# The transposed attention output: from PSUM straight into its two parts, a set at a time, and the softmax sums of a set inverted together

## The chip, the cores and the metric

The kernel runs on one core of a Trainium2 chip. The metric is the device time of one execution in microseconds. Six things work side by side on the core: TensorE (PE in the profile, with its weight loads as PEld), VectorE (DVE), ScalarE (ACT), GpSimd (POOL), SyncE (SP, which here only issues transfers) and the DMA engines. Each engine takes its instructions in the order in which they were written for it, and waits on semaphores for the others.

## What is computed

An attention with a local window of 32 keys to each side and 32 global tokens feeds a first mixture layer (the maximum of three products) and then a second one with routed experts. The change lies in the attention of the local queries. Cut to that:

```python
s_ll = scale * np.matmul(q_l, k_l.transpose(0, 1, 3, 2))      # 2 x 8 heads, 512 local queries, 64 wide
s_ll = np.where(np.abs(pos[:, None] - pos[None, :]) <= 32, s_ll, -1000000000.0)
s_lg = scale * np.matmul(q_l, k_g.transpose(0, 1, 3, 2))      # 32 global keys
a_l = sm(np.concatenate([s_lg, s_ll], axis=-1))               # e / (sum(e) + 1e-09)
out_l = np.matmul(a_l, np.concatenate([v_g, v_l], axis=2))
x = attn_out.transpose(0, 2, 1, 3).reshape(B * S, H * D)      # 1088 rows of 512
h = np.maximum(np.maximum(x @ w1, x @ w2), x @ w3)            # 512 x 768 each
x2 = h @ w_out                                                # then routed experts on x2
```

## The kernel before

**Sets and units.** The attention is cut into 16 sets `m` (a batch, a half of the sequence, a pair of heads). A set has two units, `n = 2m` and `n = 2m + 1` (called `u = 0` and `u = 1`), of 128 queries by two heads. A unit runs through: `u_scores` (PE, tile `s`), `u_max` (DVE, L183: mask, row minimum of the negated scores, tile `sm`), `u_exp` (ACT, L188, which also writes the row sums into `ssum`), `u_recip` (DVE, L192 adds 1e-9 to the unit's two sums, L193 inverts them), `u_trans` and `u_thi` (PE transposes into `pt`, ACT copies to `ph`), `u_pv` (PE, tile `pv`, then DVE scales it by the inverted sums into `xq`, L215) and `x_out`.

**What x_out does.** PE transposes the unit's `xq` into the PSUM tile `px` (128 by 128, L221). ACT copies it to `xs` in SBUF (L224). POOL rounds `xs` into `xh`, the high part of x^T (L226), and writes the rest `xs - xh` into `xl` (L227). The later matmuls work on such pairs of parts: of x^T (`xh`, `xl`), of the weights (`wh`, `wl`) and of h.

**The PSUM tile px.** Its pool `ps_x1` holds a single buffer. The transposed output, the scores of the global queries (`sgp`, from set 5 on, L240) and three tiles of a global quad (`gpt2` L266, `gpv` L277, `gpd` L282) take it in turn, each when the one before it has been read out.

**Who sets the order.** The order is written by hand: a loop over steps `s` from -2 to 37 walks through a string of pieces, one string for `s < 14` and one after it:

```python
SEQ = ('m3 scores glob max m2 w0 trans m1 pv out w1 recip quad exp w2 m0 idle',
       'w0 trans scores max pv out idle exp w1 m3 m0 quad recip m1 m2 w2 glob')
```

In step `s` the pieces stand for unit `s + 2` (`scores`, `max`, `exp`), `s + 1` (`recip`), `s` (`trans`), `s - 1` (`pv`) and `s - 2` (`out`). `glob` launches the global scores `sgp` in odd steps. `quad` carries the global quads one stage further; the quads start in steps 17, 21, 28 and 31, and their stages three, four and five later use `px` (`gpt2`, `gpv`, `gpd`). `m3`, `m0`, `m1`, `m2` are 1, 7, 4 and 2 matmuls of the first mixture layer (tile `h`, L428), which run from step 10 on where x^T and weights are there; DVE takes the running maximum of their results (`hA`, L414). `w0`, `w1`, `w2` are pieces of the splitting of the 64-bit weights: ACT `ca` (L309) and `wh` (L321), DVE L311, L314, L317, L324 and L326, and at its end POOL's `ct - wh` (L327) and `wl` (L328). `idle` are matmuls on an empty tile that keep PE busy.

After the loop, from about 116 us, come the rest of the first mixture layer, still with weights to split, its output layer, the routing and the experts.

Of the kernel before, what the change touches and what calls it, by code (L numbers as in the profile page):

```python
# [7 lines left out]
F32 = mybir.dt.float32  # L8
# [6 lines left out]
ALU = mybir.AluOpType  # L15
# [4 lines left out]
P = 128  # L20
# [26 lines left out]
def tile_block(ctx: ExitStack, tc: tile.TileContext, qk, qg, v, vo, vg, w123, w_out, w_gate, w1, w2, consts, out):  # L47
    nc = tc.nc
# [21 lines left out]
    ap = att.enter_context(tc.tile_pool(name="ap", bufs=2))  # L70
# [43 lines left out]
    ident = cst[:, 0:P]  # L114
# [36 lines left out]
    GCOL = [0, 256, 544, 832]  # L151
# [21 lines left out]
    def u_max(n):  # L173
        m, u = divmod(n, 2)
        half = SETS[m][1]
        mk = mask[:, 0 if half == 0 and u == 0 else (2 if half == 1 and u == 1 else 1), :]
        nm = ap.tile([P, 2], F32, tag="nm", bufs=4, name=f"nm{n}")
        ssum = ap.tile([P, 2], F32, tag="ssum", bufs=4, name=f"ss{n}")
        sm = sms[n % NSM]
        SM[n] = (sm, nm, ssum)  # L180
        ps = PS_.pop(n)
        for j in range(2):
            nc.vector.tensor_tensor_reduce(sm[:, j], ps[:, j, 0:P], mk, scale=-0.125, scalar=3.0e38, op0=ALU.add, op1=ALU.min, accum_out=nm[:, j : j + 1])  # L183
# [4 lines left out]
            nc.scalar.activation(sm[:, j], sm[:, j], AF.Exp, bias=nm[:, j : j + 1], scale=-1.0, accum_out=ssum[:, j : j + 1])  # L188

    def u_recip(n):  # L190
        ssum = SM[n][2]
        nc.vector.tensor_scalar_add(ssum, ssum, 1e-9)  # L192
        nc.vector.reciprocal(ssum, ssum)  # L193

    def u_trans(n):
        sm = SM[n][0]
# [371 lines left out]
    for s in range(-2, NU + 6):  # L568
        live, ahead = 0 <= s < NU, 0 <= s + 2 < NU
        if s == 10:  # L570
            mstream = Stream(moe_stream())
        pull = (lambda n: mstream.pull(n, s)) if mstream else (lambda n: None)
        nw = w_steps.get(s, 0)
        for c_ in SEQ[0 if s < 14 else 1].split():
            if c_ == "scores" and ahead:
                u_scores(s + 2)
            elif c_ == "trans" and live:
                u_trans(s)
                u_thi(s)
            elif c_ == "max" and ahead:  # L580
                u_max(s + 2)
            elif c_ == "recip" and 0 <= s + 1 < NU:
                u_recip(s + 1)
            elif c_ == "pv" and 0 <= s - 1 < NU:
                u_pv(s - 1)
            elif c_ == "out" and 0 <= s - 2 < NU:
                x_out(s - 2)
            elif c_ == "exp" and ahead:
                u_exp(s + 2)
            elif c_ == "idle":  # L590
                warm(idles.get(s, 0))
            elif c_ == "quad":
                if s in GQ:
                    globs.append(g_quad(*GQ[s]))
                globs = [g for g in globs if next(g, StopIteration) is not StopIteration]
            elif c_ == "glob" and ahead and s % 2:
                g_scores((s + 2) // 2)
            elif c_[0] == "w":
                take(ws, (nw + int(c_[1])) // 3)
            elif c_[0] == "m" and c_ != "max":  # L600
                pull(MM[int(c_[1])])

        if s % 2 == 0:
            m = (s + 6) // 2
            if 3 <= m < NSET:
                dma_qk(m)
            if 2 <= m - 1 < NSET:
                dma_v(m - 1)
        if s == 11:
            load_qg(1)  # L610
        if s + 1 in GQ:
            dma_vg(*GQ[s + 1])
        if s == 28:
            routing_start()
        if s == 30:
            nc.sync.dma_start(out.rearrange("(p i) (j c) -> p (i j) c", p=64, c=P), zero[0:64].unsqueeze(1).to_broadcast([64, NT * DM // 64 // P, P]))
# [658 lines left out]
```

## Time and profile before

| | |
|---|---|
| median of 3 timed runs | 359.81 us (359.12 to 360.7) |
| profiled execution, its own time | 356.54 us |
| span of that execution, first to last instruction | 354.8 us |
| mean granted TensorE clock | 0.987 |
| busy: PE, DVE, ACT, POOL | 325.0, 251.9, 183.5, 137.0 us |

The times of the timed runs stand some 3 us above the profiled one. Shares of busy time are averages over stages with different limits: the attention loop fills the first 116 us or so, and only that stretch is touched by the change. In the rows below a line of a timeline gives the start, the duration, the engine, the line of code, the operation with what it writes and reads, and in brackets how long the engine stood idle before it and what ended that. Matmuls are pipelined, so the durations of several can overlap.

### The profile page before, as it was taken

What the parts mean: (1) busy time and instruction counts of PE and PEld (TensorE: products, weight loads), DVE (VectorE), ACT (ScalarE), POOL (GpSimd) and SP (SyncE); (2) the same over time, 40 slices, a digit from 0 to 9 for tenths busy, and PEclk for the clock granted to TensorE, in tenths of its full rate; (3) what the DMA queues carried; (4) which work ended last, traced back from release to release, by engine and by line L of the source; (5) the groups of instructions that cost most, each with busy time, mean ns of one, the idle gap of its engine ahead of it and who ended that gap; (6) DMA issues with size and microseconds to landing.
All of it is one profiled execution on the core that took longest, in us unless ns stands there. A gap on an engine that the chain in (4) does not pass through costs nothing. (4 is left out here: it accounts for less than half of the span.)

```text
span 354.8 us, 8524 instructions
## 1 busy us (share of the span) xinstructions
PE 325.0 (92%) x3119; PEld 270.1 (76%) x3119; DVE 251.9 (71%) x665; ACT 183.5 (52%) x458; POOL 137.0 (39%) x162
## 2 busy tenths in 40 slices
PE   7989778999989999998879999999999999997990
PEld 2445546777778999998779999998987788775670
DVE  2679989975888179898973327867896955559580
ACT  3976658676664233424321113354347964768660
POOL 0377586836667156546660000400013550121121
PEclk9999989999999999999999999999999999999996
DMA  7976667752529513323100033742768997378310
GB/s 259 407 247 251 228 222 255 261 215 77 176 69 228 140 61 87 111 103 119 59 2 0 4 116 135 248 172 67 251 231 267 385 339 256 115 255 276 131 32 11
DMA packets 26294, 60.92 MB, mean 172 GB/s; under 512 B 3019, under 2 KB 8139, under 8 KB 26240
## 3 DMA queue, kind: packets, MB, share of 16 engines
q1 hardware_dynamic: 24640, 55.69, 46.3%
q0 software_dynamic: 1600, 4.54, 3.9%
q8 instruction: 30, 0.49, 0.5%
q14 instruction: 24, 0.20, 0.2%
HBM read 58.50 MB, written 7.47 MB: 186 GB/s over the span
## 5 line engine op out<-in xcount | busy, mean ns | idle before, releaser
L428 PE MATMUL h<-xh,wh 128*128 128x256 f32 (+1 forms) x288 | 85.3, 296 | 5.6 <-DVE hA L414 3.4
L428 PE MATMUL h<-xl,wh 128*128 128x256 f32 (+1 forms) x288 | 84.4, 293 | 0.0
L428 PE MATMUL h<-xh,wl 128*128 128x256 f32 (+1 forms) x288 | 84.0, 292 | 0.0
L428 PEld LDWEIGHTS h<-xh,wh 128*128 128x128 f32 x288 | 54.6, 190 | 7.6 <-DVE hA L414 4.6
L428 PEld LDWEIGHTS h<-xl,wh 128*128 128x128 f32 x288 | 54.8, 190 | 0.9 <-issue 0.7
L428 PEld LDWEIGHTS h<-xh,wl 128*128 128x128 f32 x288 | 54.7, 190 | 0.3 <-issue 0.2
L794 POOL DMA_INDIRECT xg<-x2d,idsall x12 | 14.7, 1229 | 58.6 <-DVE ordf L1150 33.3
L418 POOL TENSOR_TENSOR hTl<-hA,hTh 128x288 fp32r<-128x288 f32 (+1 forms) x18 | 15.0, 834 | 55.1 <-ACT hTh L416 55.1
L832 DVE TENSOR_TENSOR w2l<-rawb,w2h 128x1024 fp32r<-128x1024 f32 x20 | 23.9, 1223 | 12.1 <-ACT w2h L831 11.9
L928 PE MATMUL py<-w2h,hhl 128*128 128x512 f32 x112 | 30.9, 400 | 0.0
L832 DVE TENSOR_TENSOR w1l<-rawb,w1h 128x1024 fp32r<-128x1024 f32 x20 | 23.7, 1222 | 8.6 <-ACT w1h L831 8.6
L711 PE MATMUL x<-hTl,wo_h 128*128 128x256 f32 (+1 forms) x96 | 28.2, 294 | 0.0
L711 PE MATMUL x<-hTh,wo_l 128*128 128x256 f32 (+1 forms) x96 | 27.9, 290 | 0.0
L711 PE MATMUL x<-hTh,wo_h 128*128 128x256 f32 (+1 forms) x96 | 27.8, 290 | 0.0
L188 ACT ACTIVATE sm<-sm,nm 128x128 f32<-128x128 f32 x64 | 25.3, 400 | 4.7 <-DVE nm L183 4.6
L327 POOL TENSOR_TENSOR ct<-ct,wh 128x512 f32<-128x512 f32 x18 | 25.0, 1388 | 6.4 <-DVE cap L324 3.8
L226 POOL CAST xh<-xs 128x128 fp32r<-128x128 f32 x32 | 13.5, 420 | 36.0 <-ACT xs L224 36.0
L414 DVE TENSOR_TENSOR hA<-hA,h 128x256 f32<-128x256 f32 (+1 forms) x48 | 20.8, 432 | 9.2 <-PE h L428 7.2
L328 POOL TENSOR_TENSOR wl<-ct,ca 128x512 fp32r<-128x512 f32 x18 | 23.9, 1329 | 3.5 <-DVE ca L326 2.3
L416 ACT CAST hTh<-hA 128x256 fp32r<-128x256 f32 (+1 forms) x24 | 10.1, 420 | 29.3 <-DVE hA L414 29.3
L928 PEld LDWEIGHTS py<-w2h,hhl 128*128 128x128 f32 x112 | 20.9, 188 | 4.9 <-ACT hhl L916 0.4
L894 PE MATMUL acc<-w1h,xT 128*128 128x512 f32 x80 | 21.5, 399 | 1.5 <-PEq L995 0.6
(214 smaller groups left out, 757.8 us busy)
## 6 DMA issues: line engine op xcount, KB each, us to landing
rawb<-in_w_dram SPq DMA_DIRECT2D x45, 512.0 KB
raww<-in_w_dram SPq DMA_DIRECT2D x18, 512.0 KB
rawv<-in_v_dram SPq DMA_DIRECT2D x16, 512.0 KB
qk<-in_qk_dram SPq DMA_DIRECT2D x16, 320.0 KB
rawo<-in_w_out_dram SPq DMA_DIRECT2D x6, 512.0 KB
rw<-in_w_dram SPq DMA_DIRECT2D x5, 512.0 KB
out_dram<-zero SPq DMA_DIRECT2D x1, 2176.0 KB
rawg<-in_vo_dram SPq DMA_DIRECT2D x4, 512.0 KB
```

The source lines that it names most:

```text
L188: nc.scalar.activation(sm[:, j], sm[:, j], AF.Exp, bias=nm[:, j : j + 1], scale=-1.0, accum_out=ssum[:, j : j + 1])
L226: nc.gpsimd.tensor_copy(dst[0], xs)
L327: nc.gpsimd.tensor_tensor(tf, tf, hi.bitcast(F32), op=ALU.subtract)
L328: nc.gpsimd.tensor_tensor(lo, tf, b.bitcast(F32), op=ALU.add)
L414: nc.vector.tensor_tensor(hA[:, :T], hA[:, :T], ph[:, :T], op=ALU.max)
L418: eng.tensor_tensor(hl[:, f_, c0 : c0 + T], hA[:, :T], dst.bitcast(F32), op=ALU.subtract)
L428: nc.tensor.matmul(ph[:, :T], lhsT=w_[:, a], rhs=x_[:, c, c0 : c0 + T], start=n == 0, stop=n == 11)
L711: nc.tensor.matmul(po[:, :T], lhsT=w_[:, f, d * P : (d + 1) * P], rhs=h_[:, f_, c0 : c0 + T], start=k == 0, stop=k == 17)
L794: nc.gpsimd.indirect_dma_start(out=xg[t], out_offset=None, in_=src, in_offset=bass.IndirectOffsetOnAxis(ap=IDS[j][0:n, t, 0:1].bitcast(I32 ...
L832: nc.vector.tensor_tensor(l_, raw_of(j, k), h_.bitcast(F32), op=ALU.subtract)
L894: nc.tensor.matmul(ph[0:nt], lhsT=a[:, c], rhs=w_[:, c, sl], start=i == 0, stop=i == 11)
L928: nc.tensor.matmul(py[0:nt], lhsT=a[:, c, a0 : a0 + nt], rhs=w_[:, c], start=i == 0, stop=i == 23)
```

## The change

Three things change. First, `x_out` works on a set instead of a unit: in even steps it does nothing, and in odd steps it transposes both units of a set into one `px` tile of 128 by 256, and ACT copies that straight into `xh`, rounding as it writes. Second, the low part is no longer POOL's: a new function `x_low` has DVE subtract `xh` from `px` (128 by 256, both units at once). It stands at the pieces `recip`, `quad` and `glob`, and what is outstanding is done at the first of these that comes after `out`: at `recip` in the first string, at `quad` in the second. `xs` and both POOL operations are gone. `px` is now free again when DVE's subtraction has read it, where it was free after ACT's copy. Third, the sums of a set's two units lie in one tile, and both DVE operations on them run once a set, at the step where the second unit's sums are there. `xq` gets a fourth buffer, since a unit's output now waits one step longer.

```diff
     def u_recip(n):
-        ssum = SM[n][2]
-        nc.vector.tensor_scalar_add(ssum, ssum, 1e-9)
-        nc.vector.reciprocal(ssum, ssum)
+        m, u = divmod(n, 2)
+        if u == 1:
+            nc.vector.tensor_scalar_add(SS_[m], SS_[m], 1e-9)
+            nc.vector.reciprocal(SS_[m], SS_[m])
...
+    LOW = []
+
     def x_out(n):
+
         m, u = divmod(n, 2)
-        px = ps_x1.tile([P, P], F32, tag="px", name=f"pxq{n}")
-        nc.tensor.transpose(px, PV_.pop(n).rearrange("p j d -> p (j d)"), ident)
-        c0 = GCOL[m // 4] + u * P
-        xs = ap.tile([P, P], F32, tag="xs", name=f"xs{n}")
-        nc.scalar.copy(xs, px)
-        dst = [t[:, m % 4, c0 : c0 + P] for t in (xh, xl)]
-        nc.gpsimd.tensor_copy(dst[0], xs)
-        nc.gpsimd.tensor_tensor(dst[1], xs, dst[0].bitcast(F32), op=ALU.subtract)
+        if u == 0:
+            return
+        px = ps_x1.tile([P, 2, P], F32, tag="px", name=f"pxq{m}")
+        for i in range(2):
+            nc.tensor.transpose(px[:, i], PV_.pop(n - 1 + i).rearrange("p j d -> p (j d)"), ident)
+        c0 = GCOL[m // 4]
+        h_, l_ = [t[:, m % 4, c0 : c0 + 2 * P] for t in (xh, xl)]
+        px = px.rearrange("p u c -> p (u c)")
+        nc.scalar.copy(h_, px)
+        LOW.append((l_, px, h_))
+
+    def x_low():
+
+        for l_, px, h_ in LOW:
+            nc.vector.tensor_tensor(l_, px, h_.bitcast(F32), op=ALU.subtract)
+        LOW.clear()
...
-            elif c_ == "recip" and 0 <= s + 1 < NU:
-                u_recip(s + 1)
+            elif c_ == "recip":
+                x_low()
+                if 0 <= s + 1 < NU:
+                    u_recip(s + 1)
...
             elif c_ == "quad":
+                x_low()
                 if s in GQ:
...
             elif c_ == "glob" and ahead and s % 2:
+                x_low()
                 g_scores((s + 2) // 2)
```

Two places show what this does to the queues. A row gives the line (those of the changed kernel lie 3 to 25 further down), the operation, what it writes and reads, and in brackets the engine or transfer whose semaphore it waits for. The first is step 17 on DVE, between the scaling of unit 16's output (`xq16`) and the next weight piece; `hA0` is a running maximum of the first mixture layer, `gnm00` the maximum of the first global quad, `ca` the weight being split. Before:

```order
L215 TENSOR_TENSOR xq16_1076<-pv16_1067,ss16_896 128x128 [waits PE_49]
L311 TENSOR_SCALAR ca_1034<-ca_1034 128x512 [waits Activation_49]
L414 TENSOR_TENSOR hA0_0_630<-hA0_0_630,h0_0_2_874 128x256
L252 TENSOR_REDUCE gnm00_1098<-sg00_180 128x1
L253 TENSOR_SCALAR gnm00_1098<-gnm00_1098 128x1 [waits DVE_49]
L192 TENSOR_SCALAR ss18_1005<-ss18_1005 128x2
L193 RECIPROCAL ss18_1005<-ss18_1005 128x2 [waits DVE_49]
L314 TENSOR_SCALAR ca_1034<-ca_1034 128x512
```

And now:

```order
L219 TENSOR_TENSOR xq16_993<-pv16_984,ss8_830 128x128 [waits PE_49]
L326 TENSOR_SCALAR ca_952<-ca_952 128x512 [waits Activation_49]
L429 TENSOR_TENSOR hA0_0_584<-hA0_0_584,h0_0_2_808 128x256
L241 TENSOR_TENSOR xl_138<-pxq7_995,xh_137 128x256 [waits Activation_49]
L267 TENSOR_REDUCE gnm00_1014<-sg00_180 128x1
L268 TENSOR_SCALAR gnm00_1014<-gnm00_1014 128x1 [waits DVE_49]
L329 TENSOR_SCALAR ca_952<-ca_952 128x512
```

The two operations on the sums of unit 18 are gone here, and the subtraction that empties `px` (`pxq7`, set 7) stands behind the weight piece and the maximum. On PE in the same step the launch of the global scores of set 9 (`sgp9`) stands behind matmuls of `h`, before:

```order
L428 MATMUL h1_0_0_927<-xh_137,wl1_798 128x256
L428 MATMUL h1_0_1_1107<-xh_137,wh1_797 128x256
L428 MATMUL h1_0_1_1107<-xl_138,wh1_797 128x256
L428 MATMUL h1_0_1_1107<-xh_137,wl1_798 128x256 [waits Pool_49]
L240 MATMUL sgp9_1112<-qk9_809,qg1_745 64x2x160 [waits Activation_49]
L199 MATMUL pt18_1115<-cst_116,sm0_124 128x128 [waits PE_49]
```

And now:

```order
L443 MATMUL h1_0_0_855<-xh_137,wl1_736 128x256
L443 MATMUL h1_0_1_1021<-xh_137,wh1_735 128x256
L443 MATMUL h1_0_1_1021<-xl_138,wh1_735 128x256
L443 MATMUL h1_0_1_1021<-xh_137,wl1_736 128x256 [waits Pool_49]
L255 MATMUL sgp9_1026<-qk9_747,qg1_689 64x2x160 [waits DVE_49]
L203 MATMUL pt18_1029<-cst_116,sm0_124 128x128 [waits Activation_49]
```

The instructions stand alike; `sgp9` waited for ACT (the copy of `px`) and now waits for DVE (the subtraction).

The second place is step 31 on DVE, from the last sums to the weight pieces behind; `ca_` and `ct_` are two weights in the splitting, `xq30` the scaled output of unit 30. Before:

```order
L192 TENSOR_SCALAR ss31_1955<-ss31_1955 128x2
L193 RECIPROCAL ss31_1955<-ss31_1955 128x2 [waits DVE_49]
L326 SCALAR_TENSOR_TENSOR ca_1798<-raww31_1376,ca_1798 128x512
L311 TENSOR_SCALAR ca_2027<-ca_2027 128x512 [waits Activation_49,Pool_49]
L314 TENSOR_SCALAR ca_2027<-ca_2027 128x512 [waits DVE_49]
L215 TENSOR_TENSOR xq30_2079<-pv30_2070,ss30_1887 128x128 [waits PE_49]
L317 SCALAR_TENSOR_TENSOR ct_2087<-raww32_1725,ca_2027 128x512 [waits DMAHW2_49,DVE_49]
L252 TENSOR_REDUCE gnm11_2109<-sg11_1251 128x1
L253 TENSOR_SCALAR gnm11_2109<-gnm11_2109 128x1 [waits DVE_49]
L414 TENSOR_TENSOR hA2_0_1992<-hA2_0_1992,h2_0_1_2046 128x256 [waits PE_49,Activation_49,Pool_49]
```

And now:

```order
L196 TENSOR_SCALAR ss15_1751<-ss15_1751 128x4
L197 RECIPROCAL ss15_1751<-ss15_1751 128x4 [waits DVE_49]
L341 SCALAR_TENSOR_TENSOR ca_1666<-raww31_1271,ca_1666 128x512
L326 TENSOR_SCALAR ca_1875<-ca_1875 128x512 [waits Activation_49]
L329 TENSOR_SCALAR ca_1875<-ca_1875 128x512 [waits DVE_49]
L219 TENSOR_TENSOR xq30_1927<-pv30_1918,ss15_1751 128x128 [waits PE_49]
L332 SCALAR_TENSOR_TENSOR ct_1933<-raww32_1599,ca_1875 128x512 [waits DMAHW2_49,DVE_49]
L241 TENSOR_TENSOR xl_138<-pxq14_1929,xh_137 128x256 [waits Activation_49]
L267 TENSOR_REDUCE gnm11_1956<-sg11_1155 128x1
L268 TENSOR_SCALAR gnm11_1956<-gnm11_1956 128x1 [waits DVE_49]
L429 TENSOR_TENSOR hA2_0_1846<-hA2_0_1846,h2_0_1_1894 128x256 [waits PE_49,Pool_49]
```

The subtraction for set 14 (`pxq14`) stands behind four weight pieces and `xq30`. On PE in that step the fifth transpose of the third global quad (`gpt210`) takes `px`. Before:

```order
L428 MATMUL h2_0_1_2046<-xh_137,wh2_1178 128x256
L428 MATMUL h2_0_1_2046<-xl_138,wh2_1178 128x256
L428 MATMUL h2_0_1_2046<-xh_137,wl2_1179 128x256
L428 MATMUL h2_0_2_2096<-xh_137,wh2_1178 128x256 [waits DVE_49]
L265 MATMUL gpt10_2098<-cst_116,sg10_980 128x128 [waits Activation_49]
L265 MATMUL gpt10_2098<-cst_116,sg10_980 128x128 x3
L266 MATMUL gpt210_2099<-cst_116,sg10_980 32x128 [waits Activation_49]
L428 MATMUL h2_0_2_2096<-xl_138,wh2_1178 128x256
```

And now:

```order
L443 MATMUL h2_0_1_1894<-xl_138,wh2_1086 128x256
L443 MATMUL h2_0_1_1894<-xh_137,wl2_1087 128x256
L443 MATMUL h2_0_2_1942<-xh_137,wh2_1086 128x256 [waits DVE_49]
L280 MATMUL gpt10_1945<-cst_116,sg10_904 128x128 [waits Activation_49]
L280 MATMUL gpt10_1945<-cst_116,sg10_904 128x128 x3
L281 MATMUL gpt210_1946<-cst_116,sg10_904 32x128 [waits DVE_49]
L443 MATMUL h2_0_2_1942<-xl_138,wh2_1086 128x256
L443 MATMUL h2_0_2_1942<-xh_137,wl2_1087 128x256
```

`gpt210` waited for ACT and now waits for DVE, with everything behind it on PE.

## Rows read from the trace of the kernel before

**Rows 1.** Windows: busy us of each engine with instructions, granted clock, DMA share, GB/s.
```profile
40.00:50.00 10.00, 7.05 (x122) 4.53 (x122) 8.44 (x31) 7.21 (x27) 6.56 (x9) 0.92 0.64 228
50.00:60.00 10.00, 8.95 (x149) 6.30 (x141) 9.59 (x33) 6.87 (x24) 8.51 (x11) 0.91 0.94 321
60.00:70.00 10.00, 10.00 (x160) 8.00 (x160) 9.40 (x33) 7.70 (x27) 7.33 (x10) 1.00 0.61 201
```

**Rows 2.** Groups by line, 8 to 125 us: shapes, count | busy, mean ns | idle before.
```profile
L227 POOL TENSOR_TENSOR xl<-xs,xh 128x128 fp32r<-128x128 f32 x32 | 17.2, 537 | 2.6
L226 POOL CAST xh<-xs 128x128 fp32r<-128x128 f32 x32 | 13.5, 420 | 36.0 <-ACT xs L224 36.0
L192 DVE TENSOR_SCALAR ss<-ss 128x2 f32<-128x2 f32 x31 | 9.4, 303 | 0.3 <-ACT sm L188 0.2
L193 DVE RECIPROCAL ss<-ss 128x2 f32<-128x2 f32 x31 | 5.1, 166 | 1.1
L204 ACT COPY ph<-pt 128x256 f32<-128x256 f32 x32 | 11.8, 369 | 1.2 <-PE pt L199 0.7
L414 DVE TENSOR_TENSOR hA<-hA,h 128x256 f32<-128x256 f32 x12 | 5.0, 413 | 0.9 <-PE h L428 0.7 <-ACT hA L412 0.2
```

**Rows 3.** Timeline, steps 7 to 9: a weight piece on POOL, DVE behind it, PE.
```profile
22.88 1.27 POOL L328 TENSOR_TENSOR wl<-ct,ca 128x512 fp32r<-128x512 f32 x1
22.94 1.49 DVE L311 TENSOR_SCALAR ca<-ca 128x512 f32<-128x512 f32 x1
25.00 0.45 PE L171 MATMUL s<-qk 64*32 64x128 f32 x16 [1.34 <-DVE nm L183]
27.14 0.16 DVE L192 TENSOR_SCALAR ss<-ss 128x2 f32<-128x2 f32 x1
27.22 0.27 ACT L224 COPY xs<-pxq 128x128 f32<-128x128 f32 x1 [0.19 <-PE pxq L221]
```

**Rows 4.** Timeline, steps 14 and 15: the sums on DVE, the global scores on PE.
```profile
44.56 1.23 DVE L192 TENSOR_SCALAR ss<-ss 128x2 f32<-128x2 f32 x1
47.73 0.75 PE L240 MATMUL sgp<-qk,qg 128*64 128x320 f32 x2 [2.01 <-ACT xs L224]
```

**Rows 5.** Timeline, steps 17 and 18: global scores on PE, DVE, the next px.
```profile
54.39 0.75 PE L240 MATMUL sgp<-qk,qg 128*64 128x320 f32 x2 [0.29 <-ACT xs L224]
54.71 0.29 DVE L215 TENSOR_TENSOR xq<-pv,ss 128x128 f32<-128x128 f32 x1
55.71 0.41 DVE L414 TENSOR_TENSOR hA<-hA,h 128x256 f32<-128x256 f32 x1
57.01 0.33 PE L221 MATMUL pxq<-cst,xq 128*128 128x128 f32 x1 [0.76 <-ACT sg L243]
```

**Rows 6.** Timeline, step 21 (first quad's gpv) and step 27 (global scores).
```profile
68.27 0.65 PE L277 MATMUL gpv<-rawg,gph 128*32 128x64 f32 x32
68.39 0.42 DVE L414 TENSOR_TENSOR hA<-hA,h 128x256 f32<-128x256 f32 x1
91.45 0.41 DVE L414 TENSOR_TENSOR hA<-hA,h 128x256 f32<-128x256 f32 x1
91.76 0.75 PE L240 MATMUL sgp<-qk,qg 128*64 128x320 f32 x2
```

**Rows 7.** Timeline, step 31: DVE's weight pieces, gpt2 and the next pv on PE.
```profile
103.39 1.50 DVE L311 TENSOR_SCALAR ca<-ca 128x512 f32<-128x512 f32 x1
104.16 0.27 PE L266 MATMUL gpt<-cst,sg 128*32 128x128 f32 x1
106.23 0.28 DVE L215 TENSOR_TENSOR xq<-pv,ss 128x128 f32<-128x128 f32 x1
106.43 0.68 DVE L317 SCALAR_TENSOR_TENSOR ct<-raww,ca 128x512 int32<-128x512 int32 x1
106.56 0.43 PE L213 MATMUL pv<-rawv,ph 128*32 128x64 f32 x16 [1.42 <-DVE xq L215]
```

**Rows 8.** Waits after the loop, 116 to 190 us: who for whom, total us, times, longest.
```profile
DVE hA L414 <- PE h L428: 6.0, 5, 2.8
```

More of the change, by code (lines that the diff above doesn't have):

```diff
@@ L88, in tile_block @@
     SETS = [(b, half, hp) for b in range(B) for half in range(2) for hp in range(4)]
-    raws, K, V, VG, W, SG_, PV_, PS_, PT_, SM, hT = {}, {}, {}, {}, {}, {}, {}, {}, {}, {}, {}
+    raws, K, V, VG, W, SG_, PV_, PS_, PT_, SM, hT, SS_ = {}, {}, {}, {}, {}, {}, {}, {}, {}, {}, {}, {}
     def dma_qk(m):
@@ L177, in u_max @@
         nm = ap.tile([P, 2], F32, tag="nm", bufs=4, name=f"nm{n}")
-        ssum = ap.tile([P, 2], F32, tag="ssum", bufs=4, name=f"ss{n}")
+        if u == 0:
+            SS_[m] = ap.tile([P, 2, 2], F32, tag="ssum", bufs=4, name=f"ss{m}")
+        ssum = SS_[m][:, u]
         sm = sms[n % NSM]
@@ L213, in u_pv @@
                 nc.tensor.matmul(po[32 * g : 32 * g + 32, j], lhsT=ph[:, j, 32 * g : 32 * g + 32], rhs=V[m][:, 4 * u + g, 64 * j : 64 * j + 64], start=True, stop=True)
-        xq = ap.tile([P, 2, 64], F32, tag="xq", bufs=3, name=f"xq{n}")
+        xq = ap.tile([P, 2, 64], F32, tag="xq", bufs=4, name=f"xq{n}")
         nc.vector.tensor_tensor(xq, po, SM.pop(n)[2].unsqueeze(2).to_broadcast([P, 2, 64]), op=ALU.mult)
         PV_[n] = xq
+    LOW = []
     def x_out(n):
         m, u = divmod(n, 2)
-        px = ps_x1.tile([P, P], F32, tag="px", name=f"pxq{n}")
-        nc.tensor.transpose(px, PV_.pop(n).rearrange("p j d -> p (j d)"), ident)
-        c0 = GCOL[m // 4] + u * P
-        xs = ap.tile([P, P], F32, tag="xs", name=f"xs{n}")
-        nc.scalar.copy(xs, px)
-        dst = [t[:, m % 4, c0 : c0 + P] for t in (xh, xl)]
-        nc.gpsimd.tensor_copy(dst[0], xs)
-        nc.gpsimd.tensor_tensor(dst[1], xs, dst[0].bitcast(F32), op=ALU.subtract)
+        if u == 0:
+            return
[11 more added lines that the diff above has]
+        LOW.clear()
     def g_scores(m):
```

## The prediction

> **What bounds the kernel now.** I read the windows over the attention loop first [rows 1]. From 40 to 60 us DVE is busy 8.44 and then 9.59 of every 10 us and PE only 7.05 and 8.95: DVE sets the pace, and PE stands and waits. PE's granted clock is 0.92 and 0.91 there. From 60 us on PE is busy 10.00 of 10: now PE sets the pace, and any new stop of PE is paid in full. Then the groups by line [rows 2]: POOL's two operations per unit are 32 times 0.420 and 0.537 us, but POOL stood idle 36.0 us waiting for ACT before them. They are on nobody's path by themselves. What they can cost is indirect. Adding 1e-9 to two numbers on DVE (L192) takes 0.303 us in the mean and inverting the same two (L193) 0.166; one of the former took 1.23 us [rows 4]. Some DVE operations stand still while POOL works. So I looked for places where such a stop reached PE [rows 3, 4], and then for the places where PE will have to wait for DVE's new operation [rows 5 to 7].
>
> **What the change adds and removes, engine by engine.** POOL loses 13.5 + 17.2 = 30.7 us. DVE loses 16 pairs on the sums, 16 x (0.303 + 0.166) = 7.5 us, and gains 16 subtractions of 128 by 256 with one operand in PSUM. The nearest row is the running maximum of the same shape and sources, 0.413 us [rows 2], so 16 x 0.41 = 6.6 us: nearly even. ACT exchanges two copies of 0.27 us [rows 3] for one of 128 by 256, 0.369 us by L204 [rows 2], and gains 16 x 0.17 = 2.7 us that nobody waits for. PE makes the same transposes, two in a row. No transfer is issued, moved or removed. So the change is not about amounts of work but about who waits for whom.
>
> The subtraction could itself stand behind POOL. I take 0.41 for it, since L414's mean of 0.413 was taken with POOL busy beside it [rows 2]; as a bound, L192's excess over L193, 0.14 us, would come on top at each of the two places that count below, 0.3 us together. The Trainium skill (SBUF — State Buffer, Who interferes with whom) says that a VectorE instruction with at most one input in SBUF and outside the two-port modes does not contend with GpSimd, while a `tensor_scalar` can. The trace agrees (0.413 for L414, 1.23 for one L192); by the rule the sum stays as it is, without it 0.3 us are added.
>
> **The terms.** I go through the loop in time.
>
> *Step 8, a gain.* A weight piece on DVE started at 22.94, just after POOL's last weight operation (22.88, 1.27 us), took 1.49 us, and PE's next scores waited 1.34 us for DVE's maximum behind it [rows 3]. On POOL this weight stood behind `xh` and `xl` of unit 4; without their 0.42 + 0.54 us it ends before DVE comes. I take -1.2 us; the bounds are -1.34 and 0.
>
> *Steps 5 to 9, a loss.* At s = 9 DVE reaches the place where the subtraction now stands at 27.14, but ACT's copy starts at 27.22 [rows 3]. A copy of 0.37 us ends at 27.6 or later, so DVE waits some 0.45 us that it did not wait before, with the maximum of unit 11 queued behind it. DVE enters its busy stretch that much later: +0.5 us, between 0 (PE and ACT have other waits to hide it) and 1.5 (three such steps).
>
> *Steps 10 to 16, even.* At s = 15 no matmul of h stands between the transposes and `sgp`, and PE already waits 2.01 us for ACT [rows 4]. Now DVE's 0.41 us come behind ACT's copy: +0.5. Against it stands the L192 of 44.56 us, 0.9 us above its mean [rows 4], which held the chain that ACT waited for; with POOL's weight operations earlier I count half of that, -0.5. Together 0; bounds -2.0 (the whole wait goes) and +1.0.
>
> *Step 17, the first new stop.* `sgp` started at 54.39. DVE scaled `xq` only at 54.71 and took its maximum from 55.71 to 56.12 [rows 5]; the subtraction stands behind both, so it ends at 56.5 and `sgp` starts 2.1 us later. Of that comes back the 0.76 us which PE waited at 57.01 for `px` [rows 5], since even steps have no transposes now, and some 0.6 us because POOL's pieces leave DVE earlier. +0.8; bounds 0 and 2.1.
>
> *Steps 21 and 27.* `gpv` started at 68.27; the maximum that now stands ahead of the subtraction ran from 68.39 to 68.81, so `px` is free at 69.2, 0.95 us late. At s = 27 it is 91.86 + 0.41 = 92.3 against 91.76, 0.5 us [rows 6]. PE arrives later by the term above, and DVE follows PE only in part, so I take +0.5 for both; bounds 0 and 1.45. The other odd steps have DVE there in time.
>
> *Step 31, the largest.* `gpt2` ran at 104.16. The subtraction of that step stands behind three weight pieces (the second one, at 103.39, lasted 1.50 us beside POOL), `xq` at 106.23 and a fourth piece that ended at 107.11 [rows 7]. It ends at 107.5, and PE, in order, stands from 104.2 to 107.5. Part of this PE lost anyway, 1.42 us before the `pv` at 106.56 [rows 7]; but the matmuls between `gpt2` and that `pv`, which filled 104.16 to 105.14, now come after the stop: `pv` starts at 107.5 + 1.0 = 108.5 instead of 106.56, +1.9 us, less 0.2 for the transpose that step 32 no longer has. +1.7; lower bound 0.4, if DVE's pieces slip past POOL's without being held.
>
> Nothing gives this back later: after the loop DVE waits 6.0 us for PE's products [rows 8], so both engines carry a delay of PE on together.
>
> **Sum.** -1.2 + 0.5 + 0 + 0.8 + 0.5 + 1.7 = +2.3 us on the profiled execution's 356.54 us. That execution lies 3.3 us below the median of the timed runs; on their scale 359.81 + 2.3 = 362.1 us.
>
> **The rivals.** *First, the relief wins (faster).* If POOL's weight operations come so early that DVE runs ahead of PE through 40 to 60 us, the waits of 1.34, 2.01 and 0.76 us go [rows 3 to 5], 4.1 together, while the new stops shrink to 0.4 at step 31 and some 0.5 elsewhere: -3.2 us, 356.6. It decides at step 17: DVE must have done its subtraction by 54.4, over 2 us earlier than its queue allows now. For it speaks that DVE's long pieces all lie beside POOL's; against it that these are POOL's weight operations, which stay, and that small ones were only a part.
>
> *Second, no difference.* POOL's operations were hidden, DVE's amount is even, and PE's stops at 17 to 27 are filled by DVE's being earlier; then -1.2 and +1.7 remain with small change, about 360.3 us. This is also what happens if the relief does not come and the stops are shorter than I read them.
>
> *Third, the clock.* The granted clock was 0.92 and 0.91 in the windows around the 2.01 us wait of step 15 [rows 1, 4], that is, PE spent some of it at the lower of its two levels, 0.8 + 0.9 = 1.7 us lost. The new stops of 2.1 us at step 17 and 3.3 us at step 31 are as long or longer; one more such loss each gives 363.8 to 365.5 us, say 365. Against it: that the wait made the clock fall is read only from the two standing side by side, and PE had little else to do around that step, which is not so at 17 and 31. The Trainium skill (TensorE: Matmul & The Clock Gate, HAM oscillation) describes kernels in which each pause of PE throws its clock back to 1.2 GHz; by it this rival's 365 would hold, while the windows here show one such stretch in the loop.
>
> **How the numbers follow.** Forecast 0.50, with its own range of 360 to 364; relief 0.17; no difference 0.20; clock 0.13. Predicted is the forecast, 362.1 us. The range has to reach into the second and third rival: 357.8 to 366.0 leaves out most of the first, about 0.13, and a little above. A run of this kernel tells changes of about 0.5% (1.8 us) from none. Faster by more than that: the first rival, 0.17. Within it: the second mostly and the forecast's low end, 0.26. Slower: the rest, 0.57.
>
> **What would show it.** The profile after should have PE waiting for `xl` (the subtraction) at `sgp` of step 17 and, above all, some 3 us at `gpt2` near 104 us; no wait of the scores near 25 us; DVE's sums at half their count. If `gpt2` does not wait, the largest term falls and with it the sign; if PE's granted clock falls again behind step 17 or 31, the third rival holds; if DVE's subtractions start as soon as ACT's copies end from step 11 on, the first.

## The result, and the profile after

The changed kernel takes 364.44 us (median of 15 runs, 361.49 to 368.67); the kernel before, run in turn with it, 359.36 us (355.29 to 363.79). The ratio is 1.0137, 95% interval 1.0105 to 1.017: some 4.9 us slower. Single executions of one kernel differ by over 2%, so below all verdicts come from ratios of timed runs, and of a profiled execution only the order, the waits and the durations of single instructions are read. The ratios take only the executions within 1.5% of the quickest of their kernel, which leaves three of twelve for the run in which POOL subtracts from a second copy of ACT's.

First the windows over the attention loop of the kernel after (busy us of each engine with instructions, granted clock, DMA share, GB/s), to be laid beside [rows 1]:

```profile
30.00:40.00 10.00, 8.25 (x95) 5.43 (x94) 9.90 (x23) 5.03 (x20) 5.22 (x4) 0.83 0.65 226
40.00:50.00 10.00, 7.69 (x145) 5.09 (x143) 9.50 (x32) 7.68 (x26) 4.30 (x4) 1.00 0.65 228
50.00:60.00 10.00, 7.92 (x139) 5.83 (x136) 8.80 (x34) 6.79 (x23) 4.58 (x4) 1.00 0.92 324
60.00:70.00 10.00, 8.53 (x118) 6.81 (x117) 9.74 (x31) 7.50 (x26) 5.98 (x5) 1.00 0.53 197
```

PE (the first number after the window's length) was busy 10.00 of 10 us from 60 to 70 us; now it is busy 8.53 there, at the full clock of 1.00. DVE (the third) is no less busy there than before, 9.74 against 9.40. Who stops PE is told by its waits, 8 to 125 us (who for whom, total us, times, longest), of after:

```profile
PE sgp L255 <- DVE xl L241: 5.0, 3, 2.0
PE s L171 <- DVE nm L186: 2.8, 4, 1.5
PE gpt L281 <- DVE xl L241: 2.6, 1, 2.6
PE gpv L292 <- issue: 1.5, 1, 1.5
```

and the two largest of before:

```profile
PE s L171 <- DVE nm L183: 3.2, 3, 1.3
PE sgp L240 <- ACT xs L224: 2.3, 2, 2.0
```

PE waited nowhere for the low part of x^T before; now it waits 7.6 us for `xl`, in four places, and the 1.5 us at `gpv` will turn out to be a fifth. The groups by line of after, 8 to 125 us (shapes, count | busy, mean ns | idle before), answer to [rows 2]:

```profile
L241 DVE TENSOR_TENSOR xl<-pxq,xh 128x256 fp32r<-128x256 f32 x16 | 6.7, 420 | 2.2 <-ACT xh L235 1.9
L341 DVE SCALAR_TENSOR_TENSOR ca<-raww,ca 128x512 f32<-128x512 uint32 x12 | 12.2, 1017 | 0.0
L342 POOL TENSOR_TENSOR ct<-ct,wh 128x512 f32<-128x512 f32 x12 | 16.7, 1390 | 39.5 <-DVE ca L339 32.9 <-ACT wh L336 6.6
```

The subtraction takes 0.42 us. The new number is the second line: a weight piece on DVE takes 1017 ns, where before it took 817:

```profile
L326 DVE SCALAR_TENSOR_TENSOR ca<-raww,ca 128x512 f32<-128x512 uint32 x12 | 9.8, 817 | 0.0
```

And POOL now stands idle ahead of its weight operation (third line of after) until DVE has done its part, 32.9 us in all; before, it came there from its small operations, and the idle time was 0.4 us.

Where the time goes is best read from the starts of `pv`, the product that PE does once per unit (unit n is scaled in step n + 1). Each column is a kernel's start minus that of before, in us, from the timelines:

| unit | 0 | 7 | 8 | 11 | 16 | 17 | 18 | 20 | 21 | 26 | 27 | 30 | 31 | span |
|---|---|---|---|---|---|---|---|---|---|---|---|---|---|---|
| after | +0.58 | +0.98 | -0.01 | +2.30 | -0.85 | +0.94 | +0.05 | +0.08 | +1.73 | +1.75 | +3.05 | +3.02 | +4.43 | +5.0 |

The losses that stay come at three places: between units 20 and 21 (step 21), 26 and 27 (step 27), 30 and 31 (step 31). The timeline of after (start us, duration us, engine, line, instruction, in brackets the idle time before it) at step 21:

```profile
67.38 1.30 POOL L342 TENSOR_TENSOR ct<-ct,wh 128x512 f32<-128x512 f32 x1 [0.70 <-DVE ca L339]
67.58 0.28 DVE L219 TENSOR_TENSOR xq<-pv,ss 128x128 f32<-128x128 f32 x1
67.73 0.36 ACT L235 CAST xh<-pxq 128x256 fp32r<-128x256 f32 x1
67.78 1.45 DVE L341 SCALAR_TENSOR_TENSOR ca<-raww,ca 128x512 f32<-128x512 uint32 x1
69.15 0.41 DVE L429 TENSOR_TENSOR hA<-hA,h 128x256 f32<-128x256 f32 x1
69.48 0.41 DVE L241 TENSOR_TENSOR xl<-pxq,xh 128x256 fp32r<-128x256 f32 x1
70.00 0.65 PE L292 MATMUL gpv<-rawg,gph 128*32 128x64 f32 x32 [1.47 <-issue]
```

and the same place before:

```profile
67.79 0.68 DVE L326 SCALAR_TENSOR_TENSOR ca<-raww,ca 128x512 f32<-128x512 uint32 x1
67.97 0.66 POOL L226 CAST xh<-xs 128x128 fp32r<-128x128 f32 x1 [0.39 <-ACT xs L224]
68.70 0.46 POOL L227 TENSOR_TENSOR xl<-xs,xh 128x128 fp32r<-128x128 f32 x1
69.11 1.29 POOL L327 TENSOR_TENSOR ct<-ct,wh 128x512 f32<-128x512 f32 x1
```

ACT has read `px` by 68.09, but the buffer is still owed a reading by DVE. On DVE that reading stands behind a weight piece, which lasts 1.45 us instead of 0.68 because POOL's long operation started 0.40 us ahead of it; before, POOL still had its two small ones to do, and the long one came at 69.11, when DVE's piece was over. So `gpv` starts at 70.00, right after the subtraction, and not at 68.27 [rows 6]: +1.73 us. Step 27 repeats it:

```profile
92.19 1.29 POOL L342 TENSOR_TENSOR ct<-ct,wh 128x512 f32<-128x512 f32 x1 [3.88 <-DVE ca L339]
92.58 1.45 DVE L341 SCALAR_TENSOR_TENSOR ca<-raww,ca 128x512 f32<-128x512 uint32 x1
93.95 0.41 DVE L429 TENSOR_TENSOR hA<-hA,h 128x256 f32<-128x256 f32 x1
94.29 0.41 DVE L241 TENSOR_TENSOR xl<-pxq,xh 128x256 fp32r<-128x256 f32 x1
94.84 0.72 PE L255 MATMUL sgp<-qk,qg 128*64 128x320 f32 x2 [1.15 <-DVE xl L241]
```

And step 31, with the largest single stop, which answers to [rows 7]:

```profile
106.11 0.37 ACT L235 CAST xh<-pxq 128x256 fp32r<-128x256 f32 x1 [0.30 <-PE pxq L231]
108.13 1.54 DVE L332 SCALAR_TENSOR_TENSOR ct<-raww,ca 128x512 int32<-128x512 int32 x1
109.60 0.41 DVE L241 TENSOR_TENSOR xl<-pxq,xh 128x256 fp32r<-128x256 f32 x1
110.07 0.29 PE L281 MATMUL gpt<-cst,sg 128*32 128x128 f32 x1 [2.61 <-DVE xl L241]
```

ACT is done with `px` at 106.48; DVE comes to it 3.12 us later.

### The profile page after: what moved, and what is told of

It is laid out like the page before. It is cut to its first block, busy times and chain, and to the rows that moved or that the text cites. A ratio compares the mean times of both kernels' runs of the same rounds, so it can differ in the third digit from the quotient of the medians.

```text
span 359.8 us, 8419 instructions
## 1 busy us (share of the span) xinstructions
PE 327.7 (91%) x3119; PEld 272.4 (76%) x3119; DVE 249.9 (69%) x649; ACT 182.7 (51%) x442; POOL 108.7 (30%) x98
## 5 line engine op out<-in xcount | busy, mean ns | idle before, releaser
L443 PE MATMUL h<-xh,wh 128*128 128x256 f32 (+1 forms) x288 | 86.4, 300 | 4.4 <-ACT hA L427 2.2
L443 PE MATMUL h<-xl,wh 128*128 128x256 f32 (+1 forms) x288 | 85.6, 297 | 0.0
L443 PE MATMUL h<-xh,wl 128*128 128x256 f32 (+1 forms) x288 | 85.3, 296 | 0.0
L443 PEld LDWEIGHTS h<-xh,wh 128*128 128x128 f32 x288 | 55.4, 192 | 6.4 <-DVE hA L429 3.1
L433 POOL TENSOR_TENSOR hTl<-hA,hTh 128x288 fp32r<-128x288 f32 (+1 forms) x18 | 15.8, 878 | 85.7 <-ACT hTh L431 85.7
L429 DVE TENSOR_TENSOR hA<-hA,h 128x256 f32<-128x256 f32 (+1 forms) x48 | 20.8, 432 | 11.2 <-PE h L443 9.3
L186 DVE CUSTOM_DVE_ANT_0 sm<-s,mask 128x128 f32<-128x128 f32 x64 | 15.9, 286 | 12.3 <-PE s L171 12.0
```

The costliest lines, as they stand in the source:

```text
L429: nc.vector.tensor_tensor(hA[:, :T], hA[:, :T], ph[:, :T], op=ALU.max)
L433: eng.tensor_tensor(hl[:, f_, c0 : c0 + T], hA[:, :T], dst.bitcast(F32), op=ALU.subtract)
L443: nc.tensor.matmul(ph[:, :T], lhsT=w_[:, a], rhs=x_[:, c, c0 : c0 + T], start=n == 0, stop=n == 11)
```

## The experiments

The theory after this reading ("release"): `px` has one buffer, and it comes free when its last reader is done. The change makes DVE the last reader, and DVE comes late, since the subtraction stands behind weight pieces in its queue. One rival ("realignment"): the relocated work only shifts which operations meet, and any stop taken away comes back elsewhere. A second one: POOL's freedom is the cause, since its long operations now start beside DVE's weight work. A third: the sums that are inverted together cost time.

**The two parts apart.** The paired sums alone, with x^T as before:

```diff
-        ssum = ap.tile([P, 2], F32, tag="ssum", bufs=4, name=f"ss{n}")
+        if u == 0:
+            SS_[m] = ap.tile([P, 2, 2], F32, tag="ssum", bufs=4, name=f"ss{m}")
+        ssum = SS_[m][:, u]
...
-        ssum = SM[n][2]
-        nc.vector.tensor_scalar_add(ssum, ssum, 1e-9)
-        nc.vector.reciprocal(ssum, ssum)
+        m, u = divmod(n, 2)
+        if u == 1:
+            nc.vector.tensor_scalar_add(SS_[m], SS_[m], 1e-9)
+            nc.vector.reciprocal(SS_[m], SS_[m])
```

> The kernel before with the paired softmax sums alone; the x^T of a unit goes as before through ScalarE and GpSimd. Both theories (the px buffer held by VectorE's subtraction; GpSimd's products running beside VectorE's weight work) put the loss into the other part of the change, so this alone should be 0.994 to 1.004 of the kernel before, with no wait of TensorE for VectorE on px. If the pairing itself (a sum that has to wait for the second unit's exponentials) carries the loss, 1.008 or more, with xq or nm late on VectorE.

Measured: 0.992 (0.9881 to 0.9959), 356.3 us where before had 359.22. It is faster than both kernels. The third rival falls. In its waits of PE, the wait for DVE's maxima is down from 3.2 us to 0.6:

```profile
PE s L171 <- DVE nm L185: 0.6, 1, 0.6
```

Its timeline shows the wait of step 8 [rows 3] go although POOL has all its work:

```profile
22.69 0.78 DVE L314 TENSOR_SCALAR ca<-ca 128x512 f32<-128x512 f32 x1
23.26 1.34 POOL L331 TENSOR_TENSOR wl<-ct,ca 128x512 fp32r<-128x512 f32 x1
```

DVE's piece starts 0.57 us ahead of POOL's operation and lasts 0.78 us; in [rows 3] it started 0.06 us behind it and lasted 1.49.

The other part alone, x^T through ACT and DVE with the sums unit by unit:

```diff
-        if u == 0:
-            SS_[m] = ap.tile([P, 2, 2], F32, tag="ssum", bufs=4, name=f"ss{m}")
-        ssum = SS_[m][:, u]
+        ssum = ap.tile([P, 2], F32, tag="ssum", bufs=4, name=f"ss{n}")
...
-        m, u = divmod(n, 2)
-        if u == 1:
-            nc.vector.tensor_scalar_add(SS_[m], SS_[m], 1e-9)
-            nc.vector.reciprocal(SS_[m], SS_[m])
+        ssum = SM[n][2]
+        nc.vector.tensor_scalar_add(ssum, ssum, 1e-9)
+        nc.vector.reciprocal(ssum, ssum)
```

> The other half of the change alone: x^T of a set through ScalarE and VectorE as in the changed kernel, the softmax sums unit by unit as before. If the two parts simply add (sums alone 0.992, both 1.014): 1.018 to 1.026. If the sums' gain was already lost in the changed kernel, because the px waits sit where it had been, 1.010 to 1.016, as the changed kernel itself.

Measured: 1.0248 (1.0199 to 1.0296). As far as the intervals tell, the parts simply add: 0.992 x 1.0248 = 1.0166, within the interval of the whole change. So one half of the change gains some 0.8% and the other loses some 2.5%.

**Other buffers for the tiles that waited.** In the changed kernel, three tiles of the quads (the two `gpv` of the first batch element, and the `gpt2` of step 31) move from `px` to the buffer of `pt`:

```diff
-        pt2 = ps_x1.tile([P, P], F32, tag="px", name=f"gpt2{b}{quad}")
+        pt2 = (ps_t.tile([P, P], F32, tag="pt", name=f"gpt2{b}{quad}") if (b, quad) == (1, 0) else ps_x1.tile([P, P], F32, tag="px", name=f"gpt2{b}{quad}"))
...
-        pv = ps_x1.tile([P, 64], F32, tag="px", name=f"gpv{b}{quad}")
+        pv = (ps_t.tile([P, 64], F32, tag="pt", name=f"gpv{b}{quad}") if b == 0 else ps_x1.tile([P, 64], F32, tag="px", name=f"gpv{b}{quad}"))
```

> The changed kernel with three tiles of the global quads (gpt2 of the third, gpv of the first two) in the PSUM buffer of pt instead of px. Theory 'release': the waits of gpv at step 21 (1.47 us) and of gpt2 at step 31 (2.61 us, of which 1.4 cost something) go, 2.5 to 3.1 us less than the changed kernel, ratio 1.004 to 1.008. Theory 'realignment': no difference from the changed kernel, ratio 1.011 to 1.016.

Measured: 1.0031 (0.9983 to 1.0078) against 1.0137 for the changed kernel: no room for realignment's 1.011, and by its middle a little more gained than release expected. At step 21 of its timeline everything on DVE is as it was in the changed kernel, the piece of 1.45 us and the late subtraction, but `gpv` doesn't wait for it:

```profile
68.71 1.45 DVE L341 SCALAR_TENSOR_TENSOR ca<-raww,ca 128x512 f32<-128x512 uint32 x1
69.38 0.65 PE L292 MATMUL gpv<-rawg,gph 128*32 128x64 f32 x32
70.41 0.41 DVE L241 TENSOR_TENSOR xl<-pxq,xh 128x256 fp32r<-128x256 f32 x1
```

This also shows that the 1.5 us which the profile put down to "issue" at `gpv` were a wait for `px`. The control is the same move in the kernel before:

> Control: the kernel before with the same three quad tiles moved from px into the pt buffers. If the move gained in the changed kernel because VectorE no longer stops it there, it has nothing to gain here: 0.997 to 1.004. If the move is a gain of its own (px was short of buffers in both kernels), 0.986 to 0.993, as much as it gained there.

Measured: 1.0031 (0.9986 to 1.0076): nothing to gain there. The move gains only where DVE holds `px`.

Moving the global scores `sgp` instead, into the buffers of `h`, for all sets where before only the first five used them:

```diff
-        pool, tag = (ps_mm, "mm") if m < 5 else (ps_x1, "px")
+        pool, tag = (ps_mm, "mm")
```

> The changed kernel with all global scores sgp in the buffers of the h products instead of px. Theory 'release': the waits of sgp at steps 15, 17 and 27 (1.78, 2.04, 1.15 us) go; the first two stand in a stretch that DVE paces, so only step 27 and a little of 17 comes back, 1.2 to 2 us, ratio 1.008 to 1.011. Theory 'realignment': ratio 1.011 to 1.016.

Measured: 1.0158 (1.0088 to 1.0229), a miss for release and within realignment's range. Its waits of PE say where the time went:

```profile
PE sgp L255 <- DVE hA L429: 3.2, 2, 1.9
PE gpt L281 <- DVE xl L241: 2.6, 1, 2.6
```

`sgp` doesn't wait for `xl` any more; it waits for DVE all the same, since the buffers of `h` are let go by DVE's running maxima (L429). At step 17 one queue's lateness was exchanged for the same queue's lateness: 1.85 us of stop where there were 2.04. At step 27 the stop did go, but a new one of 1.31 us came at step 29, and that one goes back to a transfer: the DVE work ahead of the maximum stood behind a wait for a table of constants, 2.63 us where the changed kernel waited 0.99 for it.

```profile
101.43 0.23 DVE L145 CAST iota_b<-iota 128x128 bf16<-128x128 f32 x1 [2.63 <-DMA iota<-in_consts_dram]
```

So this run doesn't tell what the move of `sgp` is worth without that wait. Both moves together:

> Both moves together: px is used by x^T and gpd alone. Theory 'release': 4 to 5 us less than the changed kernel, ratio 0.998 to 1.003. Theory 'realignment': ratio 1.011 to 1.016.

Measured: 1.007 (1.0029 to 1.0112), between the two expectations and not better than the quads alone; the wait of 2.63 us for the constants and the stop of 1.31 us at step 29 are there as well.

**Who lets px go.** ACT makes a second copy of `px` into SBUF, and POOL subtracts from that; DVE has no part in x^T:

```diff
+        xs = ap.tile([P, 2 * P], F32, tag="xs", name=f"xs{m}")
         nc.scalar.copy(h_, px)
-        LOW.append((l_, px, h_))
+        nc.scalar.copy(xs, px)
+        nc.gpsimd.tensor_tensor(l_, xs, h_.bitcast(F32), op=ALU.subtract)
```

> The changed kernel, but ACT makes a second copy of px into SBUF and POOL subtracts from that, so px is free after ACT and DVE has no subtraction. Theory 'release' (px held by DVE's subtraction stops PE at steps 17, 21, 27 and 31): the stops of 2.04, 1.47, 1.15 and 2.61 us go, the kernel comes back to within 1.5 us of the kernel before (ratio 0.997 to 1.004). Theory 'realignment' (with POOL's small operations gone the rest of POOL's work falls on DVE's pieces at worse moments): POOL's work is back only in half, the loss of 5 us shrinks by half at most (ratio 1.006 to 1.013).

Measured: 0.9911 (0.9834 to 0.9987). The loss of the x^T part is gone, and realignment's 1.006 to 1.013 lie outside the interval. That interval is wide and reaches into release's range, so how much of the gain of the sums is left this run doesn't tell. Its longest wait of PE is for ACT again, as before:

```profile
PE sgp L257 <- ACT xs L237: 2.7, 1, 2.7
```

With the quads' move on top of it:

> The kernel with the low part by GpSimd from a second copy of ScalarE's (0.991), with the three quad tiles moved into the pt buffers as well. As px is no longer held there, the move has nothing left to gain: 0.986 to 0.996. If the quad tiles want buffers of their own whoever reads px, 0.980 to 0.986.

Measured: 0.9947 (0.9908 to 0.9986): nothing more to gain from other buffers once DVE doesn't hold `px`. And with POOL making both parts from one copy, the division of work of before but 128x256 at a time:

```diff
-        nc.scalar.copy(h_, px)
-        LOW.append((l_, px, h_))
+        xs = ap.tile([P, 2 * P], F32, tag="xs", name=f"xs{m}")
+        nc.scalar.copy(xs, px)
+        nc.gpsimd.tensor_copy(h_, xs)
+        nc.gpsimd.tensor_tensor(l_, xs, h_.bitcast(F32), op=ALU.subtract)
```

> x^T of a set in one tile, as in the changed kernel, but by the engines of before: ScalarE copies px once into SBUF, GpSimd makes the high part and the low part from the copy, 128x256 each; the sums paired. px is let go by one copy of ScalarE's. If only the reader that lets px go counts: 0.986 to 0.996, near the kernel with the paired sums alone (0.992). If working by the set is a cost of its own (the transposes of two units wait for the later one): 1.000 or more.

Measured: 0.9974 (0.9934 to 1.0013). It falls between the two expectations. Against the paired sums alone (0.992) working by the set may cost half a per cent, but the two intervals overlap, and more this run doesn't say.

The run made to part the buffer from DVE's work leaves DVE its subtraction and takes only `px` from it:

```diff
+        xs = ap.tile([P, 2 * P], F32, tag="xs", name=f"xs{m}")
         nc.scalar.copy(h_, px)
-        LOW.append((l_, px, h_))
+        nc.scalar.copy(xs, px)
+        LOW.append((l_, xs, h_))
```

> The changed kernel with one edit: ScalarE makes a second copy of px, into SBUF, and VectorE subtracts from that copy. VectorE keeps its 16 subtractions at the same places in its queue and GpSimd stays free of them; only px is now let go by ScalarE. If the px buffer held by the queued subtraction is the cause: no wait of TensorE for xl is left, and the ratio is 0.988 to 0.999. If VectorE's added work, or GpSimd's products beside its weight work, is the cause by itself: 1.008 or more.

Measured: 1.0061 (1.002 to 1.0102), between the two. No wait of PE for `xl` is left, as release wants. But the test was not clean. From SBUF eight of the 16 subtractions are lengthened, all beside an operation of POOL's (the other eight take 0.42 or 0.43 us): 802 ns in the mean where the changed kernel has 420, 16 x 0.38 = 6.1 us more on DVE. Three groups of weight pieces give some of it back (their means fall from 772 to 648, from 563 to 485 and from 1017 to 943 ns, 3.5 us together), so DVE's work grew by less; PE's waits for DVE's maxima grew from 2.8 to 4.4 us. The group of the subtraction, and one of the long ones in the timeline:

```profile
L243 DVE TENSOR_TENSOR xl<-xs,xh 128x256 fp32r<-128x256 f32 x16 | 12.8, 802 | 5.3 <-ACT xs L237 5.2
...
44.25 1.27 POOL L345 TENSOR_TENSOR wl<-ct,ca 128x512 fp32r<-128x512 f32 x1 [0.69 <-DVE ca L343]
44.48 1.33 DVE L243 TENSOR_TENSOR xl<-xs,xh 128x256 fp32r<-128x256 f32 x1 [0.37 <-ACT xs L237]
```

**The place in the queue, and POOL.** The subtraction issued directly after ACT's copy, ahead of the weight piece:

```diff
         LOW.append((l_, px, h_))
+        x_low()
```

> The changed kernel with the subtraction issued directly after ScalarE's copy, ahead of the weight piece that stood before it in VectorE's queue at steps 9, 17, 21 and others. If the place in the queue is what made px late: the waits of TensorE for xl at steps 21 and 27 (1.47 and 1.15 us) fall under 0.5, the ratio is 1.002 to 1.009. If VectorE now stands idle at the head of its queue until ScalarE's copy comes (some 0.5 to 0.6 us a set from the end of xq to the end of the copy, on 16 sets): 1.012 to 1.020, with the idle time before xl put to ACT xh.

Measured: 1.0047 (0.9999 to 1.0095): two thirds of the loss are gone. At step 21 the order is turned round:

```profile
68.30 0.42 DVE L242 TENSOR_TENSOR xl<-pxq,xh 128x256 fp32r<-128x256 f32 x1
68.64 0.90 DVE L342 SCALAR_TENSOR_TENSOR ca<-raww,ca 128x512 f32<-128x512 uint32 x1
68.78 0.65 PE L293 MATMUL gpv<-rawg,gph 128*32 128x64 f32 x32 [0.26 <-DVE xl L242]
```

From unit 20 to 21 it loses 0.44 us and from 26 to 27 0.11, where the changed kernel lost 1.65 and 1.30. The weight piece itself gains too, as it comes later against POOL's operation: 0.90 us, and over all twelve 735 ns in the mean where it was 1017. So this run moves two things at once, the release of `px` and the meeting with POOL. Of what it still loses, 1.07 us is a stop at step 29, where the subtraction stands behind the wait for the constants (2.42 us here).

Last, useless work for POOL in the changed kernel, in place of what the change took from it (21.6 us where 30.7 were taken):

```diff
         LOW.append((l_, px, h_))
+        z = ap.tile([P, 2 * P], F32, tag="xs", name=f"z{m}")
+        nc.gpsimd.tensor_copy(z, h_.bitcast(F32))
+        nc.gpsimd.tensor_tensor(z, z, h_.bitcast(F32), op=ALU.subtract)
```

> The changed kernel with useless work on GpSimd added: per set a copy and a subtraction of 128x256 into a scratch tile, about as long as the four small operations that the change took from it. px is still read by VectorE last. If GpSimd's freedom is a cause (its 512-wide products start beside VectorE's combining operation, which then takes 1.45 us where it took 0.68 at step 21, and the subtraction stands behind it): the mean of that operation falls from 1017 ns to under 900, the steps 21 and 27 lose together under 1.5 us where they lost 3.0, and the kernel with more work is the faster one, 1.005 to 1.011. If only the px buffer held by VectorE counts, it is no faster: 1.012 to 1.020.

Measured: 1.0189 (1.0121 to 1.0257), not faster than the changed kernel. Steps 21 and 27 lose less, 1.25 and 0.76 us. But from unit 14 to 15 it loses 1.25 us where the changed kernel gained 0.59, and step 31 loses 2.09. The group of the weight piece:

```profile
L344 DVE SCALAR_TENSOR_TENSOR ca<-raww,ca 128x512 f32<-128x512 uint32 x12 | 11.0, 920 | 0.0
```

The mean of the piece falls to 920 ns, not under 900. So POOL's timing decides which DVE piece is held, and with that the size of single stops; its freedom alone is not what makes the change slower, as far as work of this length shows.

What the runs settle: the loss lies in the x^T part. Three kernels spare PE the wait for DVE's late reading, each in another way: another buffer for the next tile (1.0031), an earlier release by ACT's copy (1.0061), an earlier reading (1.0047). All have intervals that end below that of the changed kernel. The first of them leaves DVE's work as it was, and its control doesn't gain. What stays open: how the 2.5% of the x^T part divide among the held buffer, DVE's added work of 6.7 us with its meetings with POOL, and working by the set. The run that was to part the first two added DVE work of its own.

## Why the prediction was right, and where not

Direction and range held: 362.1 us were predicted, with 357.8 to 366.0; on the scale of the runs that the prediction had, the ratio gives 359.81 x 1.0137 = 364.7 us. The increase was sized at 2.3 us and is 4.9. That the range held is in part luck: the forecast's own range, 360 to 364, ends below 364.7, and the wider one reached this far up for the clock's rival, which was not the cause. Term by term, from the starts of `pv`:

| term | predicted | in the trace | read from units |
|---|---|---|---|
| steps 5 to 9 | +0.5 | +0.40 | 0 to 7 |
| step 8 | -1.2 | -0.99 | 7 to 8 |
| steps 10 to 16 | 0 | -0.84 | 8 to 16 |
| step 17, with what comes back | +0.8 | +0.90 | 16 to 18 |
| steps 21 and 27 | +0.5 | +2.95 | 20 to 21, 26 to 27 |
| step 31 | +1.7 | +1.41 | 30 to 31 |

Besides, +0.58 us stood there at unit 0, ahead of every edit's effect in the prediction, and 0.6 came after unit 31; both were not foreseen. Nor was the -0.84 of steps 10 to 16. It is what is left of a swing, +2.30 us at unit 11 and -0.85 at unit 16, and TensorE's slow stretch moved with it: the granted clock is 0.83 from 30 to 40 us now, and was 0.92 and 0.91 from 40 to 60 [rows 1], 1.7 us of full clock lost both times. What made up the remainder isn't shown.

*Step 17* went as told: a stop of 2.04 us (2.1 were read from the queue). The loss from unit 16 to 17 was 1.79 us, of which 0.89 came back in the next step.

```profile
54.87 0.41 DVE L241 TENSOR_TENSOR xl<-pxq,xh 128x256 fp32r<-128x256 f32 x1
55.33 0.75 PE L255 MATMUL sgp<-qk,qg 128*64 128x320 f32 x2 [2.04 <-DVE xl L241]
```

*Step 31* had the right mechanism and nearly the right size, 2.61 us of stop, where 3.3 were read, of which 1.41 remain.

*Steps 21 and 27* are the term that was mis-sized, for two reasons that can be added. The queue of before gave 0.95 and 0.5 us, 1.45 together, and the prediction took a third of it, because "DVE follows PE only in part". It follows in full: at step 21 neither engine was later than before (`pv` by 0.08 us; `xq` at 67.58 against 67.59), and at step 27 both were by the same 1.8 us (`pv` by 1.75; the piece at 92.58 against 90.80). And the weight piece ahead of the subtraction was counted at what it took there before, 0.68 and 0.73 us; it took 1.45 in both places, 0.77 and 0.72 more. 1.45 + 0.77 + 0.72 = 2.94, against 2.95 in the trace. The bound of 1.45 on this term was too low because it priced everything but the meeting with POOL; the prediction had seen that the change makes POOL's long operations come earlier, and counted it only as relief. Over all weight pieces of DVE it is about even: the group at L326 fell from 865 ns (L311 before) to 772, that at L341 rose from 817 to 1017. But the one that rose stands ahead of the subtraction.

*Step 8* came out near its size by luck. The cause given was POOL's shorter queue: without 0.96 us of small work POOL's operation would end before DVE comes. By the prediction's own rows it would have ended at 23.19, still after DVE's 22.94 [rows 3], and in the trace it starts no earlier than before, at 22.82 against 22.88, since it now waits for DVE:

```profile
22.82 1.27 POOL L343 TENSOR_TENSOR wl<-ct,ca 128x512 fp32r<-128x512 f32 x1 [0.96 <-DVE ca L341]
24.02 0.42 DVE L326 TENSOR_SCALAR ca<-ca 128x512 f32<-128x512 f32 x1
```

DVE's piece came 1.08 us later, when POOL was as good as done, and took 0.42 us instead of 1.49. PE's scores behind it start at 25.00 in both kernels, still after a wait, of 0.61 us. So the 0.99 us are the delay of 0.98 that had grown up to unit 7, taken back, and no gain over before. With the paired sums alone and POOL's work in full, the wait goes as well: there DVE's piece came 0.25 us earlier and POOL's operation 0.38 us later, and they met in the other order.

*"Nearly even"* for DVE's amounts hid two halves that are not alike in effect: the sums taken away gain 0.8% by themselves, and the x^T part, with the subtraction put where PE waits for it, loses three times that.

*The subtraction itself* was taken at 0.41 us, unlengthened by POOL. All 16 took 0.41 to 0.43 us; eight of them lay beside an operation of POOL's for 0.37 us or more. The rule of the Trainium skill that was weighed there (SBUF — State Buffer, Who interferes with whom) is borne out by this, and by the other side of it: the same section of the Trainium skill also names a VectorE instruction with two inputs in SBUF as one that contends with a GpSimd instruction that reads SBUF, and the copy's subtraction, which has two, was lengthened eight times in 16, up to 1.50 us.

*The rivals.* Relief didn't win: the wait for ACT at step 15 [rows 4] went, and one of 1.78 us for DVE's subtraction took its place. The clock's rival wasn't seen: the granted clock is 1.00 in all windows from 40 to 70 us, around the 2.04 us stop of step 17, and 1.00 from 100 to 110 us, around the one of step 31. It was 0.83 from 30 to 40 us, ahead of all of these.

## What to carry to other kernels

When a reader of a PSUM buffer is moved to another engine, ask when that engine comes to it, not how long the reading takes: 0.42 us of work held PE for up to 2.6 us, since it stood behind weight work in that engine's queue. Cheap cures are to let a faster queue make a copy, to issue the reading ahead of the long pieces, or to give the next tile a buffer that another engine lets go; a buffer let go by the same queue may cure little (at step 17, 1.85 us of stop instead of 2.04). And measure the parts of a change apart: here one half was a gain of 0.8% that the other half hid.

## What the runs showed of the hardware

When this weight piece of DVE's, with two SBUF inputs, and a POOL operation of 128x512 meet, the later one takes longer by most of what is left of the earlier, whichever it is. In the kernel after both orders are there, 6 us apart (POOL's piece alone takes 1.28 us, DVE's 0.68):

```profile
29.57 0.68 DVE L341 SCALAR_TENSOR_TENSOR ca<-raww,ca 128x512 f32<-128x512 uint32 x1
29.60 1.78 POOL L342 TENSOR_TENSOR ct<-ct,wh 128x512 f32<-128x512 f32 x1 [5.51 <-DVE ca L339]
...
35.23 1.28 POOL L342 TENSOR_TENSOR ct<-ct,wh 128x512 f32<-128x512 f32 x1 [2.50 <-ACT wh L336]
35.28 1.77 DVE L341 SCALAR_TENSOR_TENSOR ca<-raww,ca 128x512 f32<-128x512 uint32 x1
```

A start 0.03 us ahead or 0.05 us behind decides whether DVE's piece takes 0.68 or 1.77 us. The Trainium skill (SBUF — State Buffer, Who interferes with whom) says just that, that issue order and not the operation's shape decides who is blocked. What was not expected is how much hangs on it, 1.49 of the 2.95 us at steps 21 and 27. A shift of a few hundredths of a microsecond on one engine makes a piece of the other a whole microsecond longer or shorter. In the run with POOL's useless work, which gained at two steps and lost at two others, one of the losses has this form: ahead of step 15 the sums' operation of four numbers per partition took 1.23 us beside POOL, where it took 0.16 in the changed kernel.
